# Attention and a squared-ReLU layer on one core: a buffer of its own for the last adds, GpSimd's copy behind the next sums, and DMA turns that hold back loads

## The chip, the core and the metric

The kernel runs on one core of a Trainium2 chip. Its engines are TensorE (PE; its weight loads are shown as PEld), VectorE (DVE), ScalarE (ACT), GpSimd (POOL) and SyncE (SP, which here only issues DMAs). The metric is the device time of one execution in microseconds; before the change the median of three executions was 402.41 us (402.33 to 403.97).

## The reference

Eight batches of 384 tokens go through grouped-query attention (16 query heads, 4 key/value heads, head size 64), and the result through two dense layers with a squared ReLU between them.

```python
scores = scale * np.matmul(q, k.transpose(0, 1, 3, 2))
attn = np.exp(scores - np.max(scores, axis=-1, keepdims=True))
attn = attn / (np.sum(attn, axis=-1, keepdims=True) + 1e-09)
x = np.matmul(attn, v).transpose(0, 2, 1, 3).reshape(B * S, H * D)   # 3072 x 1024
h = np.maximum(x @ w_in, 0.0)                                        # w_in 1024 x 2048
return h * h @ w_out                                                 # w_out 2048 x 1024
```

## The kernel before, in words

**A planner writes the program.** The Python code keeps a `Recorder` (lines 9 to 145). Every operation is added with the keys that it reads and writes and with an estimated cost; the recorder keeps a clock for each engine and derives the semaphore waits. The main loops (from line 1701 for batches 0 and 1, from line 1856 for the others) look at these clocks and choose what TensorE does next. Before each choice `upkeep` (line 1624) looks which side work is due: loads, DMA turns, sums, squares, output writes. So the order of every queue comes from estimated times, and a changed estimate can change the order of later work.

**The stages of a batch.** Loads of k, q and v go through POOL's queue (`load_k`, `load_q`, `load_v`). SP issues DMA transposes ("turns") of k and q (`turn_k_half`, `turn_q_dma`). Scores come in bursts of matmuls (line 448), ACT applies exp (line 458), TensorE multiplies by v (line 515), DVE divides by the sum (lines 528 and 530), and a DMA turn of the outputs (`turn_o_dma`, line 533) makes `xT`, the input of the dense layers. For batches 2 to 7 both dense layers use seven block products in place of eight (Strassen). DVE makes the sums of `xT` that this needs (`sums`, line 649, instructions at line 658); then TensorE runs the upward products (line 902) while the attention of the next batch goes between them. The results are added on DVE (line 886), and squared into `h2T` by ACT (lines 788, 796) or by POOL (line 800, in `close_squares`).

**The downward products.** Rows of 128 tokens are paired. Each batch has three such rows; two make pair "A", and the third one is paired with the third row of the batch before (pair "D" of the odd batches). For that, POOL copies the third row's part of `h2T` into `h2x` in batches 2, 4 and 6 (line 1199, queued in `d_q` by `sum_ops`, line 1151; `d_q` is a queue in order). Each pair runs seven products (line 944, in `pair_of`). As products end, `done` (line 1108) evicts them: `copied` makes a copy on ACT (line 1094) or DVE (line 1095), `added` adds on DVE (line 1101), and at product 7 POOL adds two buffers, `p5 += a3` (line 1133). `put` queues the output's DMA on SP (line 1308). The buffers `y_sb` are slots handed out in turn by `y_slot`. In the last pair the products end in the order 7, 4, 3, and product 3 runs as `whole_product` (line 999): first 384 columns, then 128.

**Pacing.** For batches above 3, `dma_at` holds the time before which no further load piece (2.0 after the one before) or turn of k, v or q (3.5 after) may be issued (lines 1651 and 1660). The turns of outputs are not paced.

**DVE and POOL.** An operation with `port=True` is one for which the planner charges more when POOL is at work (line 87): it adds the time by which the two overlap, over POOL's last four operations. `w2_q` (line 1692) places the scaling and the sums of the second weight matrix (lines 1226, 1231, 1238) on DVE or ACT as their planned clock is within `lead` of TensorE's.

Of the kernel before, what the change touches and what calls it, by code (L numbers as in the profile page):

```python
# [8 lines left out]
class Recorder:  # L9
# [36 lines left out]
    def add(self, eng, fn, reads=(), writes=(), dma=None, cost=0.1, issue=0.1, shared=(), after=(), port=False):  # L46
        i = len(self.ops)
        deps = self.deps_of(reads, writes)
        raw = {self.writer[r] for r in reads if r in self.writer}
        for r in reads:  # L50
            self.readers.setdefault(r, []).append(i)
        for w in writes:
            self.writer[w] = i
            self.readers[w] = []
        need = set(after)
        for d in deps:
            o = self.ops[d]
            if o["dma"] is None and o["eng"] == eng and dma is None:
                if eng in self.IN_ORDER or d not in raw:
                    continue  # L60
            need.add(d)
        if dma is not None:
            if dma in self.dma_last:
                need.add(self.dma_last[dma])
            self.dma_last[dma] = i
        start = max([self.clock[eng]] + [self.ops[d]["end"] for d in need])
        if dma is not None:
            self.clock[eng] = start + issue
            if eng == "gpsimd":
                self.pool.append((start, start + 0.3 * issue))  # L70
            q = eng
            begin = max(self.ring.get(q, 0.0), start + issue + 0.8)
            if shared and begin > start + issue + 0.8:
                shared = (3.0, shared[1])
            if shared and self.ring.get("gpsimd", 0.0) > begin:
                self.ring["gpsimd"] += shared[1]
                for o in self.ops:
                    if o["eng"] == "gpsimd" and o["dma"] is not None and o["end"] > begin:
                        o["end"] += max(0.0, min(shared[1], o["end"] - 1.2 - begin))
                cost = shared[0]  # L80
            self.ring[q] = begin + cost
            end = begin + cost + (1.5 if begin > 30 else 1.2 if eng == "gpsimd" else 0.7)
        else:
            if eng == "gpsimd":
                self.pool.append((start, start + cost))
            elif port:
                cost += 1.0 * sum(max(0.0, min(z, start + cost) - max(a, start)) for a, z in self.pool[-4:])
            self.clock[eng] = start + cost
            end = start + cost + (0.2 if eng == "tensor" else 0.07)
        self.ops.append(dict(eng=eng, fn=fn, dma=dma, need=need, signal=False, start=start, end=end))  # L90
        return i
# [57 lines left out]
def bass_gqa_attention__then__ffn_squared_relu_kernel(  # L149
# [619 lines left out]
    def close_squares(which):  # L769

        for x in [x for x in open_squares if which(x)]:
            open_squares.remove(x)
            i, r, dst, keys, relu, b = x
            assert b < FAST or b in ranged
            val = hr[r]
            two = val.rearrange("p (f t) -> p f t", f=2)
            end = R.ops[i]["end"]
            act, dve, pool = [max(R.clock[e], end) for e in ("scalar", "vector", "gpsimd")]
            slack = 1.5 * (b >= FAST and keys[0][1:] not in LAST_SQUARES)
            plans = [(act + 0.45 * (1 + relu) + slack, "ss"), (max(act + 0.52 * relu, pool) + 0.77 + 0.2, "sg")]  # L780
            if relu:
                plans.append((pool + 2.2 + 0.6, "gg"))
            elif not ff["now"]:
                plans.append((dve + 0.95 + 0.4, "sv"))
            one, other = min(plans)[1]
            to, by = small(b)
            if relu and one == "s":
                R.add("scalar", lambda e, val=val, to=to: e.activation(val, val, AF.Relu, scale=to),  # L788
                      reads=[("hr", r)] + by, writes=[("hr", r)], cost=0.54 if by else 0.45)
            elif relu:  # L790
                R.add("gpsimd", lambda e, val=val, to=to: e.tensor_scalar(val, val, to, 0.0, ALU.mult, ALU.max),
                      reads=[("hr", r)] + by, writes=[("hr", r)], cost=1.42)
            for _, c, t in keys:
                wrote[c, t] = b
            if other == "s":
                R.add("scalar", lambda e, dst=dst, two=two: e.activation(dst, two, AF.Square),  # L796
                      reads=[("hr", r)], writes=keys, cost=0.45)
            else:
                eng = dict(g="gpsimd", v="vector")[other]
                n = R.add(eng, lambda e, dst=dst, two=two: e.tensor_tensor(dst, two, two, ALU.mult),  # L800
                          reads=[("hr", r)], writes=keys, cost=0.77 if other == "g" else 0.95, port=other == "v")
                if other == "v":
                    hr_read[r] = (n,)

# [249 lines left out]
    def pair_of(b, pair, one, two):  # L1054
# [28 lines left out]

        ys = {}
        g1, g2 = b_1 % 3, b_2 % 3

        def slot(name):
            ys[name] = y_slot(b)
# [15 lines left out]
        def put(who, x, name, c0=0, c1=512):  # L1104
            bb, i3 = who
            send(bb, i3, 512 * x + c0, 512 * x + c1, ys[name], c0)

        def done(prod, at, *cols):
            flags.add(("done", b, pair, prod))
            if prod == 1:  # L1110
                copied(at, "a1", g1)
            elif prod == 2:
                added(at, g1, "a1", "a1")
                put(one, 0, "a1")
            elif prod == 5:
                copied(at, "p5", g2)
                ys["bank"] = at
            elif prod == 6:
                eng = copied(at, "a2", g2)
                if g1 != g2:  # L1120
                    copied(at, "b2", g1, eng)
                else:
                    ys["b2"] = ys["a2"]
                if b == B - 1 and pair == "D":
                    added(ys["bank"], g1, "b2", "b2", TAIL, 512, (R.writer[("y", ys["p5"])],))
            elif prod == 7:
                if g1 == g2:
                    slot("a3")
                else:
                    ys["a3"] = ys["a2"]  # L1130
                added(at, g2, "a2", "a3")
                y, z = ys["a3"], ys["p5"]
                R.add("gpsimd", lambda e: e.tensor_tensor(y_sb[z], y_sb[z], y_sb[y], ALU.add),
                      reads=[("y", y), ("y", z)], writes=[("y", z)], cost=1.28)
                put(two, 1, "p5")
            elif prod == 3:
                added(at, g1, "b2", "b2", *cols)
                put(one, 1, "b2", *cols)
            else:
                added(at, g2, "a3", "a3")  # L1140
                put(two, 0, "a3")

        def product(prod, at):
            (a, na), (w, nw) = left(prod), right(prod)
# [6 lines left out]
    def sum_ops(b, double):  # L1151
# [40 lines left out]
        if double:  # L1192
            for n, prod in ((0, 5), (1, 6), (3, None), (2, 3)):
                reads, go = op("D", n, None)
                d_q.append((lambda prod=prod: prod is None or ("done", b, "A", prod) in flags, reads, go, True))
        elif b < B - 1:
            keys = [("h2T", c, 1) for c in range(NFC)] + [("DS", b, "A", n, x) for n in (2, 3) for x in range(2)]
            d_q.append((lambda: all_wrote(range(NFC), (1,)), keys, lambda: R.add(
                "gpsimd", lambda e: e.tensor_copy(h2x[:, :, :], h2_16[:, :, 256:384]), reads=keys,
                writes=[("h2x", b), ("h2x", b - 2)] + X_OVER, cost=2.0), True))  # L1200

# [325 lines left out]
    def below():  # L1527
        return not ff["tiles"] and not ff["now"]
# [95 lines left out]
    def upkeep(now):  # L1624
# [66 lines left out]
            add_sums(b)  # L1691
        while w2_q and w2_q[0][0]() and R.when(reads=w2_q[0][1], eng="none") <= now:
            eng = w2_q[0][3]
            lead = {"scalar": 0.6 if ff["b"] == 1 else 0.1, "vector": 0.5 if ff["b"] == FAST and not below() else -9 if m_q or lazy else 0.6 if below() else 0.9 if ff["b"] == 1 else 0.1}
            able = [x for x in ("vector", "scalar") if eng in (x, "any") and R.clock[x] <= now + lead[x]]
            if not able:
                break
            w2_q.pop(0)[2](*(able[:1] if eng == "any" else ()))
# [157 lines left out]
    while ff["now"] or ff["tiles"] or ff["down"]:  # L1856
# [60 lines left out]
        elif what[2] == "av2":  # L1917
# [7 lines left out]
                    m_q.append((b, lambda b=b: widest_of(b)))  # L1925
            if c % 2 == 1:
                turn_o_dma(b, c // 2)
                x_done[b] += 2
        elif what[2] == "top":
            n, then = spread_q.pop(0)  # L1930
# [39 lines left out]
```

## Time and profile before

| what | value |
|---|---|
| median of three executions | 402.41 us |
| the profiled execution's own time | 402.27 us |
| its span, first to last instruction | 400.3 us |
| PE busy | 389.6 us (97%) |
| DVE busy | 315.4 us (79%) |
| ACT busy | 266.7 us (67%) |
| POOL busy | 148.4 us (37%) |
| granted TensorE clock | 0.999 |

The span leaves out 1.97 us of the profiled execution's own time, which lie before the first or after the last instruction. In rows of the timeline the first number is the start in microseconds from the span's beginning, the second the duration; x2 means that two such instructions are merged into one row, and what stands in square brackets is the engine's idle time before it and what ended it. A matmul's end is modelled, and TensorE works on several at a time, so that "busy" is not the same as full speed.

### The profile page before, as it was taken

The page shows a single profiled execution, that of the slowest core. Times are in us where ns is not written, and L with a number is a line of the kernel's source. Part 1 is how long each engine was busy: PE and PEld are TensorE (multiplying, and loading weights), DVE is VectorE, ACT ScalarE, POOL GpSimd, SP SyncE. Part 2 cuts the span into 40 slices and gives each one's busy share as a digit, 9 for nine tenths or more (in the row PEclk, how much of TensorE's full clock was granted, in tenths as well). Part 3 has the DMA queues.
Part 4 walks back from the last instruction along what each step waited for, and adds up shares of the span by engine and source line. Part 5 has one row for each costly group of instructions (what it writes and reads, how often), then busy time and mean ns, then how long its engine had stood idle before and what let it go on. Part 6 is the DMA issues. An engine that isn't in the chain of part 4 may idle for free.

```text
span 400.3 us, 15645 instructions
## 1 busy us (share of the span) xinstructions
PE 389.6 (97%) x7022; PEld 300.2 (75%) x7022; DVE 315.4 (79%) x652; ACT 266.7 (67%) x390; POOL 148.4 (37%) x169
## 2 busy tenths in 40 slices
PE   9999999999999999999999999998999999999995
PEld 6565764555666897588977999698987899789653
DVE  3689879899898987987987788986885688856644
ACT  6948999596655897768675587877783297426510
POOL 8665510245001664355332343444301144126111
PEclk9999999999999999999999999999999999999999
DMA  9999999995329873398597816697622223120022
GB/s 174 189 199 182 207 185 190 208 165 80 43 75 189 133 86 60 76 179 91 99 120 161 162 23 92 81 149 109 70 60 93 92 44 25 48 80 4 28 81 104
DMA packets 95634, 44.39 MB, mean 111 GB/s; under 512 B 75984, under 2 KB 89552, under 8 KB 95568
## 3 DMA queue, kind: packets, MB, share of 16 engines
q0 software_dynamic: 36672, 17.44, 35.6%
q1 hardware_dynamic: 58224, 25.47, 31.9%
q8 instruction: 55, 0.90, 1.0%
q10 hardware_dynamic: 672, 0.49, 0.4%
q14 instruction: 11, 0.09, 0.1%
HBM read 35.65 MB, written 12.58 MB: 121 GB/s over the span
## 4 chain that ended last, share of the span: by engine, by line
PE 78%; DVE 7%; DMA 7%; issue 4%; POOL 3%; ACT 1%; POOLq 0%; ACTq 0%; DVEq 0%
PE ps L944 27%; PE ps L902 26%; PE ps L515 6%; PE ps L448 6%; PE ps L611 6%; DMA w_in_sb<-in_moe_w_in_dram 5%; PE ps L1276 5%; DMA wx<-in_k_dram 1%; PE ps L474 1%; DVE w_out_sb L1226 1%; POOL w_in_sb L320 1%; DVE hr L624 1%; DVE y_sb L1101 1%; DVE w_out_sb L1238 1%; ACT h2T L796 1%
## 5 line engine op out<-in xcount | busy, mean ns | idle before, releaser
L458 ACT ACTIVATE expT<-ps 128x1024 bf16<-128x1024 f32 (+1 forms) x124 | 120.8, 1015 | 25.3 <-PE ps L448 25.2
L944 PE MATMUL ps<-w_out_sb,h2T 64*128 64x512 f16 x528 | 97.8, 376 | 0.5 <-DVE y_sb L1101 0.5
L902 PE MATMUL ps<-xT,w_in_sb 64*128 64x192 f16 x1152 | 84.8, 243 | 0.3 <-DVE y_sb L1101 0.3
L902 PEld LDWEIGHTS ps<-xT,w_in_sb 64*128 64x128 f16 x1152 | 71.2, 94 | 3.5 <-DVE y_sb L1101 0.5
L800 POOL TENSOR_TENSOR h2T<-hr 128x384 f16<-128x384 f32 x54 | 44.6, 845 | 51.7 <-ACT hr L788 51.6
L944 PE MATMUL ps<-area,xT 64*128 64x512 f16 x288 | 55.8, 376 | 0.0
L944 PEld LDWEIGHTS ps<-w_out_sb,h2T 64*128 64x128 f16 (+1 forms) x528 | 41.1, 94 | 15.8 <-DVE y_sb L1101 0.6
L448 PE MATMUL ps<-qT,kT 64*128 64x256 bf16 (+2 forms) x336 | 51.4, 326 | 0.6 <-ACT expT L458 0.4
L902 PE MATMUL ps<-s_all,wx 64*128 64x192 f16 x768 | 51.9, 242 | 0.0
L788 ACT ACTIVATE hr<-hr,bits 128x384 f32<-128x384 f32 x71 | 41.9, 609 | 11.8 <-DVE hr L886 11.5
L886 DVE TENSOR_TENSOR hr<-ps,hr 128x384 f32<-128x384 f32 x72 | 39.2, 555 | 9.4 <-PE ps L902 6.2
L902 PEld LDWEIGHTS ps<-s_all,wx 64*128 64x128 f16 x768 | 44.4, 94 | 0.9
L515 PE MATMUL ps<-v_aug,expT 64*128 64x65 bf16 x1680 | 43.7, 190 | 1.2 <-issue 0.6
L611 PE MATMUL ps<-xT,w_in_sb 64*128 64x384 bf16 x448 | 42.1, 323 | 1.0 <-DVE hr L624 0.6
L1101 DVE SCALAR_TENSOR_TENSOR y_sb<-ps,bits,y_sb 128x512 f32<-128x512 f32 (+2 forms) x38 | 26.9, 724 | 19.9 <-PE ps L944 13.3
L515 PEld LDWEIGHTS ps<-v_aug,expT 64*128 64x128 bf16 x1680 | 39.3, 94 | 2.7 <-DVE o_sb L530 0.7
L944 PE MATMUL ps<-area,h2T 64*128 64x512 f16 x144 | 36.4, 376 | 0.0
L1094 ACT ACTIVATE y_sb<-ps,bits 128x512 f32<-128x512 f32 x20 | 13.6, 687 | 33.7 <-PE ps L944 33.6
L878 ACT COPY hr<-ps 128x384 f32<-128x384 f32 x34 | 16.2, 479 | 27.2 <-PE ps L902 26.6
L611 PEld LDWEIGHTS ps<-xT,w_in_sb 64*128 64x128 bf16 x448 | 22.0, 94 | 16.2 <-DVE hr L624 1.8
L902 PE MATMUL ps<-s_all,w_in_sb 64*128 64x192 f16 x384 | 32.8, 243 | 1.3 <-issue 1.3
L902 PE MATMUL ps<-xT,wx 64*128 64x192 f16 x384 | 33.2, 243 | 0.7 <-issue 0.6
(147 smaller groups left out, 748.6 us busy)
## 6 DMA issues: line engine op xcount, KB each, us to landing
out_dram<-y_sb SPq DMA_DIRECT2D x45, 256.0 KB, 2.4
w_in_sb<-in_moe_w_in_dram POOLq DMA_DIRECT2D x8, 512.0 KB, 15.1
w_out_sb<-in_moe_w_out_dram POOLq DMA_DIRECT2D x4, 1024.0 KB, 28.9
q_st<-in_q_dram POOLq DMA_DIRECT2D x19, 192.0 KB, 5.2
q_st<-in_q_dram POOLq DMA_DIRECT2D x4, 384.0 KB, 23.1
k_st<-in_k_dram POOLq DMA_DIRECT2D x6, 192.0 KB, 4.1
k_st<-in_v_dram POOLq DMA_DIRECT2D x5, 192.0 KB, 5.0
wx<-in_q_dram POOLq DMA_DIRECT2D x2, 384.0 KB, 8.4
```

Of the source, the lines that this page charges most:

```text
L448: mm = pe.matmul(ps[:, base + x, m * wide:(m + 1) * wide], kT[at(b)][64 * x:64 * x + 64, u, :], q_cols(b, u // NJ, x, c0, c0 + wide))
L458: R.add("scalar", lambda e: e.activation(dst, src, AF.Exp, scale=0.125), reads=keys, writes=[("expT", slot(b, u), t) for u, _, _ in pieces ...
L515: m = pe.matmul(ps[:, p[x], n * DP:n * DP + D + 1], w, v_aug[b % 2][r, g * NJ + j, 0:D + 1], start=(n + j + y == 0), stop=(n + j + y == 2 ...
L611: m = pe.matmul(bank(4 + xs[x])[:, 0:S], w_in_sb[r, kc, c * 128:(c + 1) * 128], xT[b % NXT][r, kc, :], start=(phase < 2 and kc == 0), stop ...
L788: R.add("scalar", lambda e, val=val, to=to: e.activation(val, val, AF.Relu, scale=to), reads=[("hr", r)] + by, writes=[("hr", r)], cost=0. ...
L800: n = R.add(eng, lambda e, dst=dst, two=two: e.tensor_tensor(dst, two, two, ALU.mult), reads=[("hr", r)], writes=keys, cost=0.77 if other ...
L878: R.add("scalar", lambda e: e.copy(hr[r][:, :], src), reads=[("bank", at)], writes=[("hr", r)], cost=0.45, after=hr_read.pop(r, ()))
L886: R.add("vector", lambda e: e.tensor_tensor(hr[r][:, :], src, hr[r][:, :], ALU.add), reads=[("bank", at), ("hr", r)], writes=[("hr", r)], ...
L902: return lambda pe: pe.matmul(bank(at)[:, f * h:f * h + h], w[r, kc, c:c + 128], m[r, kc, :], start=(prod in (1, 5, 2) and y + f + kc == 0 ...
L944: return lambda pe: pe.matmul(bank(p.at)[:, 0:512], p.a(k, r), p.w(k, r), start=start, stop=stop, skip_group_check=True)
L1101: R.add("vector", lambda e: e.scalar_tensor_tensor(y_sb[z][:, c0:c1], bank(at)[:, c0:c1], gs[g], y_sb[y][:, c0:c1], ALU.mult, ALU.add), re ...
L1276: m = pe.matmul(bank(i)[:, 0:n], h2T[:, c, i3 * 128:(i3 + 1) * 128], w_out_sb[:, c, c0:c1], start=(c == 0), stop=(c == NFC - 1))
```

## The change

Six things change, all in the planner's code.

1. The charge for `port=True` operations (line 87): instead of the overlap with POOL's last four operations it is the rest of that POOL operation (of the last six) which is running when the DVE operation starts.
2. A square on POOL or DVE gets a wait on earlier instructions of the same engine that read the part of `h2T` which it overwrites.
3. In the last pair alone (`last`): the two copies at product 6 go to ACT, and the add of product 4 writes a new slot `a4` and no longer overwrites `a3`, which POOL's add reads.
4. The copy into `h2x` becomes due only when the sums of the next batch are made.
5. `lead` for `w2_q` on DVE in batch 1 falls from 0.9 to 0.5 while the upward products run.
6. In the loop for batches 2 to 7, each turn of outputs moves `dma_at` to at least 3.5 after TensorE's clock, so that no load piece and no paced turn follows earlier.

```diff
@@ Recorder.add
             elif port:
-                cost += 1.0 * sum(max(0.0, min(z, start + cost) - max(a, start)) for a, z in self.pool[-4:])
+                cost += max([0.0] + [z - start for a, z in self.pool[-6:] if a <= start < z])
@@ close_squares
                 n = R.add(eng, lambda e, dst=dst, two=two: e.tensor_tensor(dst, two, two, ALU.mult),
-                          reads=[("hr", r)], writes=keys, cost=0.77 if other == "g" else 0.95, port=other == "v")
+                          reads=[("hr", r)], writes=keys, cost=0.77 if other == "g" else 0.95, port=other == "v",
+                          after=tuple(d for key in keys for d in R.readers.get(key, ()) if R.ops[d]["eng"] == eng))
@@ pair_of
+        last = b == B - 1 and pair == "D"
...
-                eng = copied(at, "a2", g2)
+                eng = copied(at, "a2", g2, "scalar" if last else None)
...
-                if b == B - 1 and pair == "D":
+                if last:
                     added(ys["bank"], g1, "b2", "b2", TAIL, 512, (R.writer[("y", ys["p5"])],))
...
-                added(at, g2, "a3", "a3")
-                put(two, 0, "a3")
+                ys["a4"] = slot("a4") if last else ys["a3"]
+                added(at, g2, "a3", "a4")
+                put(two, 0, "a4")
@@ sum_ops
-            d_q.append((lambda: all_wrote(range(NFC), (1,)), keys, lambda: R.add(
+            d_q.append((lambda: b + 1 in summed and all_wrote(range(NFC), (1,)), keys, lambda: R.add(
                 "gpsimd", lambda e: e.tensor_copy(h2x[:, :, :], h2_16[:, :, 256:384]), reads=keys,
@@ upkeep
-            lead = {"scalar": 0.6 if ff["b"] == 1 else 0.1, "vector": 0.5 if ff["b"] == FAST and not below() else -9 if m_q or lazy else 0.6 if below() else 0.9 if ff["b"] == 1 else 0.1}
+            lead = {"scalar": 0.6 if ff["b"] == 1 else 0.1, "vector": 0.5 if ff["b"] == FAST and not below() else -9 if m_q or lazy else 0.6 if below() else 0.5 if ff["b"] == 1 else 0.1}
@@ loop for batches 2 to 7
                 turn_o_dma(b, c // 2)
+                dma_at[0] = max(dma_at[0], R.clock["tensor"] + 3.5)
                 x_done[b] += 2
```

## The prediction

> **What bounds the kernel now.** I read the page first: the span, the busy times, and the chain of work that ended last.
>
> ```profile
> span 400.3 us, 15645 instructions
> PE 389.6 (97%) x7022; PEld 300.2 (75%) x7022; DVE 315.4 (79%) x652; ACT 266.7 (67%) x390; POOL 148.4 (37%) x169
> PE 78%; DVE 7%; DMA 7%; issue 4%; POOL 3%; ACT 1%; POOLq 0%; ACTq 0%; DVEq 0%
> ```
>
> TensorE is busy for 389.6 of 400.3 us, and the change takes no matmul away. So what can be won is mostly the 10.7 us in which TensorE does nothing. Asked for by window, the last stretch holds almost half of them.
>
> ```profile
> 371.00:401.00 30.00, 25.05 (x233) 14.33 (x228) 14.19 (x24) 6.22 (x11) 3.12 (x3) 0.97 0.20 71
> ```
>
> The first number behind the stretch is its length, the second PE's busy time: 4.95 us without work, of which 0.7 lie past the span's end. For the rest I asked whom PE waited for (total us, times, longest).
>
> ```profile
> PE ps L902 <- issue: 2.0, 2, 1.3
> PE ps L611 <- DVE hr L624: 0.6, 2, 0.4
> PE ps L515 <- issue: 0.6, 1, 0.6
> PE ps L515 <- DVE o_sb L530: 0.5, 1, 0.5
> PE ps L944 <- DVE y_sb L1101: 0.5, 1, 0.5
> ```
>
> So the middle has two kinds of holes: 2.6 us of "issue", where PE waits for nothing that the profile shows, and 1.6 us behind a late DVE. Anything else that the change moves is under a busy PE.
>
> **Part 3, the last pair.** This is the end of the timeline, with the issue times of the output DMAs and the adds by form.
>
> ```profile
> 393.52 1.03 DVE L1101 SCALAR_TENSOR_TENSOR y_sb<-ps,bits,y_sb 128x128 f32<-128x128 f32 x2
> 394.13 1.92 PE L999 MATMUL ps<-w_out_sb,xT 128*128 128x384 f16 x16
> 394.63 1.27 POOL L1133 TENSOR_TENSOR y_sb<-y_sb 128x512 f32<-128x512 f32 x1 [10.82 <-DVE y_sb L1101]
> 395.92 2.64 SPq L1308 DMA_DIRECT2D out_dram<-y_sb  x4
> 396.00 1.73 DVE L1101 SCALAR_TENSOR_TENSOR y_sb<-ps,bits,y_sb 128x512 f32<-128x512 f32 x3 [1.45 <-POOL y_sb L1133]
> L1101 DVE SCALAR_TENSOR_TENSOR y_sb<-ps,bits,y_sb 128x384 f32<-128x384 f32 x1 | 0.6, 609 | 0.0
> L1308 SPq DMA_DIRECT2D out_dram<-y_sb x4: 332/332/432, 395.9 to 398.1; - x4
> ```
>
> DVE is free at 394.55 but waits 1.45 us until POOL has read `a3`; then three adds run one after the other until 397.73 (0.75 for the whole width, 0.61 for 384 columns, the rest, some 0.35, for 128), and the last DMA is issued by 398.56. With a slot of its own the add of product 4 starts at about 394.6 and ends at 395.3. The 384-column add follows its matmuls, whose share of the 1.92 us is 384/512, 1.44: it runs from about 395.6 to 396.2. The last add comes after all matmuls (396.05) and that one: 396.2 to 396.55, 1.2 us earlier than 397.73. On SP the output of `a4` is ready first (395.3), then POOL's (395.9), then the other two: three issues of 0.33 and one of 0.43 behind 395.92 at most, so that the last ends at about 397.0 in place of 398.56, 1.5 us earlier. The same 768 KB then leave in less time, so I take **-1.4**. Bounds: -0.9 if POOL's output is issued ahead of `a4` and all four issues take 0.43 (395.92 + 1.73 = 397.65, against 398.56), and -1.55.
>
> This needs DVE's add to run beside POOL's. An earlier pair shows just that.
>
> ```profile
> 382.55 1.26 POOL L1133 TENSOR_TENSOR y_sb<-y_sb 128x512 f32<-128x512 f32 x1 [10.96 <-DVE y_sb L1101]
> 383.44 0.75 DVE L1101 SCALAR_TENSOR_TENSOR y_sb<-ps,bits,y_sb 128x512 f32<-128x512 f32 x1 [0.98 <-PE ps L944]
> 390.35 0.69 ACT L1094 ACTIVATE y_sb<-ps,bits 128x512 f32<-128x512 f32 x1 [2.77 <-PE ps L944]
> 392.07 1.41 DVE L1095 TENSOR_SCALAR y_sb<-ps,bits 128x512 f32<-128x512 f32 x2 [2.70 <-PE ps L944]
> ```
>
> The add begun at 383.44 took 0.75, its usual time, while POOL worked until 383.81. The two copies moved to ACT cost twice 0.69 in place of 1.41 and end at the same time; ACT's row behind it shows 2.77 us of idle time, so they cost **0**. Without that cover the first add would be late by what they take longer.
>
> **Part 4, the copy behind the sums.** Batch 4's copy lies like this.
>
> ```profile
> 252.91 1.90 POOL L1199 COPY area<-h2T 128x2048 f16<-128x2048 f16 x1
> 253.07 1.83 DVE L675 CAST top_w<-bits 128x128 bf16<-128x128 f32 x1
> 254.82 0.74 DVE L1101 SCALAR_TENSOR_TENSOR y_sb<-ps,bits,y_sb 128x512 f32<-128x512 f32 x1
> L675 DVE CAST top_w<-bits x14: 226/227/1829, 57.6 to 346.6; 128x128 bf16<-128x128 f32 x14
> ```
>
> The cast takes 0.227 as a rule and 1.83 here, to the end of the copy. The add of line 1101 behind it comes 1.6 us late, and PE waits 0.5 for that add. Behind the sums the cast has long run, and the next squares come only with the next upward products. I take **-0.5**, the whole wait. Who waits for the copy: POOL's own queue (q loads, `p5` adds) and pair D's first products, more than a batch's upward products later. In batch 2 it can hit something new:
>
> ```profile
> 167.59 0.55 DVE L658 TENSOR_TENSOR s_all<-xT,s_all 128x768 f16<-128x768 f16 x1
> 168.90 1.25 POOL L1133 TENSOR_TENSOR y_sb<-y_sb 128x512 f32<-128x512 f32 x1 [0.47 <-DVE y_sb L1101]
> 169.03 1.21 DVE L675 CAST top_w<-bits 128x128 bf16<-128x128 f32 x1
> ```
>
> A copy from 168.2 would keep this cast until 170.1, or, with POOL's add behind it, until 171.4; now it ends at 170.24. The scale that hangs on it is needed only at the seventh piece of the next upward products, so I count 0, with +0.6 as the upper bound.
>
> **Parts 1 and 5, DVE's planned clock.** Two places with several `port` operations in a row (the first in batch 1, where `lead` is changed, the second in batch 2):
>
> ```profile
> 88.80 4.37 DVE L1226 TENSOR_SCALAR w_out_sb<-w_out_sb,bits 128x1024 f16<-128x1024 bf16 x6
> 135.73 2.55 DVE L1238 TENSOR_TENSOR w_out_sb<-w_out_sb 128x1024 f16<-128x1024 f16 x2
> 135.75 1.99 POOL L338 COPY k_dup<-k_st 128x1536 bf16<-128x1536 bf16 x1
> ```
>
> The six of line 1226 hold DVE until 93.17, and one of the two waits for line 624 quoted above ends behind them. The two sums of line 1238 took 2.55 us, since the second stood until POOL's copy ended at 137.74. The old charge can at most double such an operation; the new one charges the whole rest, as the cast above shows it. With that and the smaller `lead`, fewer of them are put ahead of the adds that PE waits for. The price is in the waits quoted first: 0.6 for line 624 and 0.5 for line 530, 1.1 in all. The operations have to go somewhere, so I take a third, **-0.4**, with -1.1 and +1.1 (as much again in new places) as bounds.
>
> **Part 6, the held-back loads and turns.** The largest "issue" hole, with the DMAs ahead of it; of a window's last two numbers the first is the mean busy share of the DMA engines, which passes 1 where queues overlap.
>
> ```profile
> 266.46 2.06 SPq L535 DMA_TRANSPOSE xT<-o_sb  x1
> 267.34 0.74 POOL L302 DMA_DIRECT2D k_st<-in_v_dram  x1 [3.91 <-PE ps L448]
> 270.80 1.70 SPq L362 DMA_TRANSPOSE qT<-q_st  x1
> 270.00:272.00 2.00, 2.00 (x62) 1.93 (x58) 1.66 (x4) 1.08 (x3) 0.29 (x1) 1.00 1.36 238
> 273.31 1.33 issue
> q8 instruction: 55, 0.90, 1.0%
> ```
>
> PE stops in the middle of one product without a semaphore, in a stretch where a turn of outputs, a load and a turn of q overlap. Its instructions come by DMA too (55 packets, 0.90 MB), and I read the hole as instructions that came late. With the hold, the load at 267.34 (0.9 us after the turn) moves back by up to 2.6 us, and the q turn behind it by as much. That may free this hole, but the loads then meet the next fetch. I take about a quarter of 2.6, **-0.6**; the bounds are -2.6 and +1.3, one more hole of the longest kind. In its section "Queues, rings and completion order" the Trainium skill's page "DMA: Bandwidth & Descriptors" says that a DMA engine takes turns between its queues packet by packet; by that a fetch waits for a few packets and not for whole transfers, and the hold would win nothing here (a rival below). No row here settles it.
>
> **Part 2, waits of POOL on itself,** cost **0**: what they wait for, POOL's own sums and copies of the batch before, ended long ago, and POOL sits idle for 51.7 us ahead of these squares.
>
> ```profile
> L800 POOL TENSOR_TENSOR h2T<-hr 128x384 f16<-128x384 f32 x54 | 44.6, 845 | 51.7 <-ACT hr L788 51.6
> ```
>
> All 54 could start 0.95 later (51.7 / 54) and that idle time would still take it, in the mean.
>
> **The sum**: -1.4 - 0.5 - 0.4 - 0.6 = -2.9. The profiled execution took 402.27, so 399.4; the median of the runs is 0.14 above it, which gives **399.5**.
>
> **The rivals.** *The end alone.* The plan is made anew, and the holes in the middle only change places: -1.4, or -1.9 with the cast, 400.5 to 401.0. For it speaks that the middle's holes are small and follow from chance meetings; against it that the cast and the doubled sums have a plain cause. *The holds win nothing at the "issue" holes:* instructions are late for a reason of their own, since two of the three holes are only 0.6 long and stand in other stretches; then -2.3, 400.1. *The holds eat the slack (slower).* Batch 5's first q turn is issued at 187.34 and its first exp runs at 201.85.
>
> ```profile
> 187.34 1.86 SPq L362 DMA_TRANSPOSE qT<-q_st  x1
> 201.85 1.94 ACT L458 ACTIVATE expT<-ps 128x1024 bf16<-128x1024 f32 x2 [1.25 <-PE ps L448]
> DMA to landing us min/median/max: 3.7/4.0/4.3
> ```
>
> With 4.0 us to land, 10.5 us are free. Four turns of outputs per batch hold 3.5 each, 14 at most; past 10.5 the scores come late and PE has nothing to put between the downward products. At 14 that is 3.5 us in batch 5, and 402.4 - 1.4 + 3.5 = 404.5, more if later batches follow. Against it: most turns lie closer together with what follows than 3.5, but a hold runs at the same time as the 2.0 and 3.5 that are kept already. *The change does not do what it says.* If the add of product 4 still ends behind POOL's, the end wins 0.2 at most, and all else is chance: 402.
>
> **How the numbers follow.** I count 0.5% (2.0 us) as what can be told from no change: below 400.4 is faster, above 404.4 slower. The forecast case has 0.38 (its own range is 397.0 to 400.4), the holds without gain 0.12, the end alone 0.28, the holds that eat the slack 0.15, the change without effect 0.07. Faster is the first two, 0.50; same is 0.28 + 0.07 less 0.02 for new holes that cost more, 0.33; slower 0.17. The range reaches from 397.0, where the fetch term and the clock term are near their lower bounds, to 403.5, which takes in the rivals but the holds in full.
>
> **What would show it.** Right: DVE's add of product 4 begins near 394.6 on the old scale, with no wait for POOL at line 1101, and the span ends some 1.4 us sooner after the last matmul than now; no cast over 0.3 beside line 1199; "issue" under 2.6 in PE's waits; fewer doubled sums at lines 1226 to 1238. Wrong: a new row in PE's waits behind exp or `qT`, or "issue" holes of the same total elsewhere.

## The result, and the profile after

The changed kernel took 399.41 us (median of 6 runs, 398.96 to 401.24) against 402.37 of the kernel before on the same chip (6 runs): a ratio of 0.9932, 95% interval 0.9908 to 0.9956, or 3.0 us less. The prediction was 399.5.

The profiled execution is the longest of these six, 401.24. The same kernel was profiled a second time, at 399.02; its span there is 397.2. Of the runs in the table further down, one (405.94, with the copy alone) lies 1.6% above the shortest of its kernel, at a granted clock of 0.992, and is left out. First the page of the changed kernel: span, busy times, chain of work.

```profile
span 399.4 us, 15634 instructions
PE 388.2 (97%) x7019; PEld 298.7 (75%) x7022; DVE 313.1 (78%) x645; ACT 272.4 (68%) x398; POOL 147.6 (37%) x168
PE 85%; DMA 7%; DVE 3%; POOL 2%; issue 1%; ACT 1%; POOLq 0%; DVEq 0%
```

TensorE bounds it as before; DVE's and issue's shares of the chain fell from 7% to 3% and from 4% to 1%. Most of the 4% was no idle time of TensorE: the chain of the kernel before ended through POOL's last add, and 10.79 us of "issue" at 383.81 are POOL's time ahead of it. Whom PE waited for (total us, times, longest), in the changed kernel:

```profile
PE ps L903 <- issue: 2.4, 3, 1.1
PE ps L448 <- ACT expT L458: 1.5, 4, 0.5
PE ps L611 <- DVE hr L624: 0.9, 2, 0.7
```

and in the second profile of it:

```profile
PE ps L448 <- ACT expT L458: 1.7, 5, 0.5
PE ps L903 <- issue: 0.6, 2, 0.4
```

Three things are to be seen. Two waits of 0.5 each are gone, that of line 515 behind line 530 and that of the downward products behind the add of line 1101 (now 1103). The wait behind exp has grown from 0.4 to 1.5 and 1.7. And two executions of one program differ by 1.8 us in the "issue" row alone, where their times differ by 2.2: these holes make up most of the difference between these two, so a single profile says little about them.

The end of the changed kernel, in the timeline and by its output writes:

```profile
392.21 1.27 ACT L1096 ACTIVATE y_sb<-ps,bits 128x512 f32<-128x512 f32 x2 [1.04 <-PE ps L945]
393.51 2.02 DVE L1103 SCALAR_TENSOR_TENSOR y_sb<-ps,bits,y_sb 128x128 f32<-128x128 f32 x3 [4.00 <-ACT y_sb L1096]
394.26 1.92 PE L1000 MATMUL ps<-w_out_sb,xT 128*128 128x384 f16 x16
394.77 1.27 POOL L1135 TENSOR_TENSOR y_sb<-y_sb 128x512 f32<-128x512 f32 x1 [10.82 <-DVE y_sb L1103]
395.77 1.07 DVE L1103 SCALAR_TENSOR_TENSOR y_sb<-ps,bits,y_sb 128x384 f32<-128x384 f32 x2 [0.25 <-PE ps L1000]
L1311 SPq DMA_DIRECT2D out_dram<-y_sb x4: 332/332/450, 395.6 to 397.2; - x4
DMA to landing us min/median/max: 1.8/2.0/2.2
```

The third of the three adds merged at 393.51 is that of product 4; it runs beside POOL's add and waits for nothing. The last matmuls end at 396.18 and the span at 399.4: 3.2 us, against 4.2 before (396.05 and 400.3). The longer stretch that the prediction began with now reads

```profile
371.00:401.00 30.00, 25.18 (x235) 14.68 (x231) 13.07 (x22) 7.63 (x13) 3.26 (x3) 0.98 0.20 72
```

4.82 us without PE's work, of which 1.6 lie past the span's end (0.7 before).

### The profile page after: what moved, and what is told of

The parts are those of the page before. It is cut to its first block, busy times and chain, and to the rows that moved or that the text cites. A ratio compares the mean times of both kernels' runs of the same rounds, so it can differ in the third digit from the quotient of the medians.

```text
span 399.4 us, 15634 instructions
## 1 busy us (share of the span) xinstructions
PE 388.2 (97%) x7019; PEld 298.7 (75%) x7022; DVE 313.1 (78%) x645; ACT 272.4 (68%) x398; POOL 147.6 (37%) x168
## 4 chain that ended last, share of the span: by engine, by line
PE 85%; DMA 7%; DVE 3%; POOL 2%; issue 1%; ACT 1%; POOLq 0%; DVEq 0%
PE ps L945 32%; PE ps L903 28%; PE ps L515 7%; PE ps L448 6%; PE ps L611 5%; DMA w_in_sb<-in_moe_w_in_dram 5%; PE ps L1279 5%; DMA area<-in_v_dram 1%; DVE hr L624 1%; PE ps L474 1%; DVE w_out_sb L1229 1%; POOL w_in_sb L320 1%; ACT expT L458 1%; DVE y_sb L1103 0%; POOL q_st L309 0%
## 5 line engine op out<-in xcount | busy, mean ns | idle before, releaser
L945 PE MATMUL ps<-w_out_sb,h2T 64*128 64x512 f16 x528 | 96.2, 376 | 0.0
L800 POOL TENSOR_TENSOR h2T<-hr 128x384 f16<-128x384 f32 x50 | 40.5, 829 | 47.1 <-ACT hr L788 46.9
L945 PE MATMUL ps<-area,xT 64*128 64x512 f16 x288 | 54.3, 376 | 0.0
L448 PE MATMUL ps<-qT,kT 64*128 64x256 bf16 (+2 forms) x336 | 50.4, 324 | 1.8 <-ACT expT L458 1.5
L945 PEld LDWEIGHTS ps<-w_out_sb,h2T 64*128 64x128 f16 (+1 forms) x528 | 38.7, 94 | 17.2 <-ACT h2T L796 0.3
L515 PE MATMUL ps<-v_aug,expT 64*128 64x65 bf16 x1680 | 42.7, 190 | 0.1
L1096 ACT ACTIVATE y_sb<-ps,bits 128x512 f32<-128x512 f32 x24 | 16.3, 687 | 38.1 <-PE ps L945 35.2
L1135 POOL TENSOR_TENSOR y_sb<-y_sb 128x512 f32<-128x512 f32 x9 | 12.1, 1346 | 79.5 <-DVE y_sb L1103 79.5
```

Of the source, the lines that this page charges most:

```text
L448: mm = pe.matmul(ps[:, base + x, m * wide:(m + 1) * wide], kT[at(b)][64 * x:64 * x + 64, u, :], q_cols(b, u // NJ, x, c0, c0 + wide))
L515: m = pe.matmul(ps[:, p[x], n * DP:n * DP + D + 1], w, v_aug[b % 2][r, g * NJ + j, 0:D + 1], start=(n + j + y == 0), stop=(n + j + y == 2 ...
L945: return lambda pe: pe.matmul(bank(p.at)[:, 0:512], p.a(k, r), p.w(k, r), start=start, stop=stop, skip_group_check=True)
```

## The experiments

All ratios are to the kernel before on the same chip; 1% is 4.0 us, and gains in us below are worked out from the ratios.

| kernel | median us (runs) | before us | ratio, 95% interval |
|---|---|---|---|
| end alone (part 3) | 401.32 (12) | 402.15 | 0.9981, 0.9957 to 1.0004 |
| hold alone (part 6) | 403.43 (12) | 402.15 | 1.0032, 1.0008 to 1.0055 |
| plan alone (parts 1, 5) | 403.10 (12) | 402.15 | 1.0011, 0.9984 to 1.0037 |
| copy alone (parts 4, 2) | 400.70 (9) | 402.15 | 0.9960, 0.9939 to 0.9981 |
| all, second profile | 399.00 (6) | 402.38 | 0.9930, 0.9905 to 0.9955 |
| all but the hold | 399.76 (12) | 402.38 | 0.9947, 0.9925 to 0.9969 |
| copy and end, early write | 401.52 (12) | 402.38 | 0.9986, 0.9960 to 1.0011 |
| before, small loads and turns | 397.92 (5) | 402.38 | 0.9912, 0.9883 to 0.9940 |
| before, small turns alone | 401.14 (12) | 401.94 | 0.9978, 0.9957 to 1.0000 |
| plan and hold | 400.18 (12) | 401.94 | 0.9945, 0.9923 to 0.9967 |
| all, third write by itself | 399.34 (8) | 401.94 | 0.9943, 0.9921 to 0.9966 |
| all, hold of 7.0 | 434.28 (6) | 401.94 | 1.0791, 1.0759 to 1.0823 |

### The parts one by one

The end alone:

```diff
+                ys["a4"] = slot("a4") if last else ys["a3"]
+                added(at, g2, "a3", "a4")
+                put(two, 0, "a4")
```

> The kernel before with part 3 alone (the last pair's copies on ACT, the add of product 4 into a slot of its own). My theory: only the end changes, and the span ends about 1.0 us sooner after the last matmul than before (4.25 us before, 3.2 us in the changed kernel's profile), so the time falls by 0.9 to 1.4 us. The rival that the end wins next to nothing, because the outputs then leave in a bunch, expects less than 0.4 us.

The median went down by 0.8, the ratio's interval reaches from -1.7 to +0.2. In its trace the span ends 3.2 us after the last matmul, as in the whole change, against 4.2 before: the traces show a gain of 1.0 at the tail, smaller than the 1.4 forecast, which the runs alone do not tell from nothing.

The hold alone:

```diff
                 turn_o_dma(b, c // 2)
+                dma_at[0] = max(dma_at[0], R.clock["tensor"] + 3.5)
```

> The kernel before with part 6 alone (each turn of outputs of batches 2 to 7 holds back loads and paced turns by 3.5). My prediction gave -0.6 us (fewer holes of the 'issue' kind). Rival one, the holes come whatever the loads do: 0 +-0.5. Rival two, the holds eat the slack: over +1 us, with waits for exp or for qT in PE's list.

It made the kernel slower, by 1.3 (0.3 to 2.2). Its profiled execution is its shortest of twelve (401.67), and even that has one "issue" hole of

```profile
PE ps L515 <- issue: 1.6, 1, 1.6
```

The exp wait stays at 0.4 here, so late scores are not what it paid for. Part of the 1.3 is a lower granted clock in 7 of its 12 runs (below, under "Do the parts add up?").

The plan alone (the new charge and the lead):

```diff
+                cost += max([0.0] + [z - start for a, z in self.pool[-6:] if a <= start < z])
...
-  else 0.9 if ff["b"] == 1 else 0.1}
+  else 0.5 if ff["b"] == 1 else 0.1}
```

> The kernel before with parts 1 and 5 alone (the charge for DVE operations beside POOL, the smaller lead in batch 1). My prediction gave -0.4 us, by fewer waits of PE for lines 624 and 530 (1.1 us before). The rival that the new plan only moves the holes expects 0, and the waits for DVE as long as before in other places.

No gain in the median: +0.4 (-0.6 to +1.5), with a lower granted clock in 8 of its 12 runs (below). In its trace the wait behind line 530 is gone, but the one behind line 624 has grown from 0.6 to 0.9, and there is an "issue" row of 2.7:

```profile
PE ps L902 <- issue: 2.7, 2, 2.5
PE ps L611 <- DVE hr L624: 0.9, 2, 0.7
```

The copy alone:

```diff
-            d_q.append((lambda: all_wrote(range(NFC), (1,)), keys, lambda: R.add(
+            d_q.append((lambda: b + 1 in summed and all_wrote(range(NFC), (1,)), keys, lambda: R.add(
```

> The kernel before with parts 4 and 2 alone (the copy into h2x due only after the next sums; POOL's waits on itself). My prediction gave -0.5 us. The profile of the changed kernel speaks for a rival: POOL's queue runs ahead of the plan, nothing in the program makes the copy wait for the sums, and so it starts when POOL is free; then it lies at the same place as before (about 252.9 in batch 4, beside the cast) and the time stays within 0.3 us.

It gained 1.6 (0.8 to 2.5), more than the 0.5 of the hole. This is the group of casts and batch 4's copy in its timeline:

```profile
L675 DVE CAST top_w<-bits x14: 226/227/228, 56.2 to 345.4; 128x128 bf16<-128x128 f32 x14
252.78 0.23 DVE L675 CAST top_w<-bits 128x128 bf16<-128x128 f32 x1
257.04 0.55 DVE L658 TENSOR_TENSOR s_all<-xT,s_all 128x768 f16<-128x768 f16 x1
259.16 1.90 POOL L1200 COPY area<-h2T 128x2048 f16<-128x2048 f16 x1
```

The copy runs behind the sums, no cast is held up, and the wait of PE for line 1101's add has gone. In the changed kernel the same places look like this:

```profile
252.18 0.68 DVE L1183 TENSOR_TENSOR xT<-h2T,xT 128x1024 f16<-128x1024 f16 x1
252.93 1.89 POOL L1202 COPY area<-h2T 128x2048 f16<-128x2048 f16 x1 [4.67 <-DVE xT L1183]
254.02 0.88 DVE L675 CAST top_w<-bits 128x128 bf16<-128x128 f32 x1
256.75 0.54 DVE L658 TENSOR_TENSOR s_all<-xT 128x768 f16<-128x768 f16 x1
```

The copy starts 3.8 us *ahead* of the sums. The edit moves its place in POOL's queue, and no wait ties it to the sums; with the hold, the loads that stood ahead of it in that queue come later, so POOL reaches the copy as soon as the last sum of line 1183 is there. Without the hold (all but the hold, below) it lies behind the sums again, at 258.94, and the longest cast takes 0.255. The cast still meets it, for 0.88 in place of 1.83, because the copy now begins 0.07 us behind that sum, where before it began 1.0 behind it (252.91, and the sum's end at 251.92). That is short enough: PE no longer waits for the add behind it. For this part 4 is not needed. The plan with the hold (below) has no part 4, and its copy too begins 0.07 us behind the last sum (250.33 + 0.68), its longest cast is the same, and the downward products' wait of 0.5 behind line 1101 is gone there too:

```profile
250.33 0.68 DVE L1180 TENSOR_TENSOR xT<-h2T,xT 128x1024 f16<-128x1024 f16 x1
251.08 1.89 POOL L1199 COPY area<-h2T 128x2048 f16<-128x2048 f16 x1 [4.67 <-DVE xT L1180]
252.17 0.88 DVE L675 CAST top_w<-bits 128x128 bf16<-128x128 f32 x1
```

### Do the parts add up?

The four ratios give -0.8, +1.3, +0.4 and -1.6, together -0.7; the whole gives -2.8. So parts were put together.

> The changed kernel once more, for a second profile and to stand beside the next three on one chip. Expected: -2.7 us +-1 against the kernel before; its waits of PE behind exp (1.5 us near 168 in the first profile) belong to the plan and come again at the same place, while the 'issue' holes near 186, 196 and 275 come at the same places with other lengths.

The wait behind exp came again near 168. Of the "issue" holes of the first profile, the one near 186 did not, the one near 195 came with 0.37 in place of 0.90, and the one near 274 with 0.2 in place of 1.05.

> The changed kernel without part 6 (no hold behind the turns of outputs). If the hold costs what it cost alone (+1.3 us), this is faster than the changed kernel by 0.5 to 2 us. If it pays only together with the other parts (the prediction's -0.6), this is slower than the changed kernel by 0.5 or more. With POOL's loads back ahead of the copy in its queue, the copy of batch 4 should then lie behind the cast again, as it does with part 4 alone.

All but the hold is at 0.9947, where the sum of its parts by themselves is -2.0, 0.9950: these three add up. With the hold it is 0.9930. The intervals overlap, so this pair alone doesn't show that the hold is worth anything; the spread of the runs is narrower with it (398.42 to 399.12 in six, against 397.94 to 401.37 in twelve).

The pair that shows a difference is the plan without and with the hold:

> Parts 1, 5 and 6 alone, without the end and the copy. Theory, hold and new plan gain together though each alone gained nothing: the median is that of the whole change plus what the end (1.0) and the copy's hole (0.5) are worth, about 400.5. Rival, the parts add up as measured one by one (+0.4 and +1.3): 403.5 to 404.

Each of them alone was no faster than before; together they are faster by 2.2 (1.3 to 3.1), and the interval lies clear of that of the plan alone. Added up they would be 1.7 slower. Its waits:

```profile
PE ps L448 <- ACT expT L458: 1.7, 5, 0.5
PE ps L902 <- issue: 1.0, 1, 1.0
```

It has the new wait behind exp, which neither part shows alone (0.2 to 0.4 in both), and less "issue" than either. So the two medians do not add up.

Most of that gap goes with the clock. For every run the mean granted clock is on record, the share of its full clock that TensorE got:

| kernel | runs at 0.996 or less | their median | median of the others |
|---|---|---|---|
| before, beside the first four rows | 0 of 33 | | 402.15 |
| hold alone | 7 of 12 | 404.28 | 402.46 |
| plan alone | 8 of 12 | 403.61 | 400.93 |
| before, beside plan and hold | 3 of 25 | 404.49 | 401.62 |
| plan and hold | 0 of 12 | | 400.18 |

One profile has a mean of 0.996, that of the end alone (403.71). An "issue" hole of 2.29 us ends there at 183.56, and from 184.82 on the clock is at 0.50 for 3.41 us. The third number from the end is the clock:

```profile
181.30:183.50 2.20, 0.00 (x0) 0.00 (x0) 0.40 (x1) 1.44 (x3) 1.69 (x3) 1.00 1.03 85
185.00:188.00 3.00, 3.00 (x39) 3.00 (x37) 1.87 (x4) 1.76 (x3) 1.62 (x2) 0.50 0.41 41
```

At half the clock 3.41 us lose 1.7, which is 0.4% of the run, as the mean says. Not every such hole brings this: behind the one of 2.50 of the plan alone, the clock stays at 1.00. Among the runs without it the plan is 1.2 faster than before, the hold 0.3 slower, and both together are 1.4 faster. That is near a sum, but the groups are small and chosen by what came of them, so no part's price is shown by it. What the pair has and neither part alone has is a trace without a hole from 172 to 184, where the plan alone has its 2.50 and the hold alone its 1.6. Why the two together avoid it was not found out.

### What makes the "issue" holes

The kernel before, with a quarter of the rows in each load of k, v and q and one block in each turn of k and q, in batches 4 to 7 only:

```diff
-            q_st[st][:, h0:h1, :],
+            q_st[st][:, h0:h0 + 1 if b > 3 else h1, :],
...
-            out=qT[at(b)][:, 12 * half:12 * half + 12, :],
+            out=qT[at(b)][:, 12 * half:12 * half + (1 if b > 3 else 12), :],
...
```

> The kernel before with the same plan and the same instructions, but of batches 4 to 7 each load of k, v and q brings only a quarter of its rows and each turn of k and q turns only one block of 6 or 12: what these batches compute is left wrong, the turns of outputs and all else is as before. If the 'issue' holes come from instructions that wait behind loads and turns, the holes near 177, 182 and 274 (2.6 us together in the profile before) go and the time falls by 1.5 to 3 us. If a fetch is late for its own reasons (queues served in turn, packet by packet), the holes stay and the time stays within 0.5 us.

The kernel leaves out most of the input of these batches, so it only serves to time the rest. It took 3.5 us less (2.4 to 4.7), and no "issue" row is left in PE's waits. The order of every engine's instructions is that of the kernel before, so only the DMA traffic differs. PE's busy time in the middle, first before and then with small loads and turns (stretch, its length, PE's busy time; the last two numbers are the DMA share and GB/s):

```profile
160.00:280.00 120.00, 117.00 (x2512) 99.22 (x2512) 98.49 (x216) 86.00 (x119) 50.30 (x56) 1.00 0.73 112
```

```profile
160.00:280.00 120.00, 119.87 (x2627) 102.84 (x2625) 101.28 (x222) 87.88 (x122) 48.13 (x58) 1.00 0.31 65
```

2.9 us of PE's idle time have gone; 2.5 of them are the three "issue" holes (0.56, 0.65 and 1.33), and the wait of 0.5 behind line 1101 has gone too. What comes late can be seen in the DMA queues of 6 us ahead of the largest hole (packets, MB, share of 16 engines). In the kernel before, from 266 to 272:

```profile
q1 hardware_dynamic: 1849, 0.92, 92.2%
q0 software_dynamic: 589, 0.22, 35.7%
...
k_st<-in_v_dram POOLq DMA_DIRECT2D x1, 192.0 KB, 7.0
xT<-o_sb SPq DMA_TRANSPOSE x1, 7.7
qT<-q_st SPq DMA_TRANSPOSE x1, 4.7
```

With small loads and turns, the same stretch:

```profile
q0 software_dynamic: 144, 0.05, 9.5%
q1 hardware_dynamic: 315, 0.06, 6.4%
q8 instruction: 2, 0.03, 2.9%
...
xT<-o_sb SPq DMA_TRANSPOSE x1, 2.8
```

Two instruction packets (queue q8) pass with small loads, none in the kernel before. That kernel runs some us behind by then, so the packets are better compared by their number: both kernels have 55, and the 37th starts at 272.32 in the kernel before, 6.6 us after the 36th (265.71), and at 266.56 with small loads, 4.3 after it (262.25). It comes 2.3 us later than there. It ends at 273.30, and PE, which stops at 273.31, goes on at 274.64, 1.3 us behind that end. The same is seen at all 22 "issue" holes of over 0.3 us in the twelve traces that have one: each ends 1.3 to 1.6 us after the end of this queue's last packet, and it is always the 21st, 22nd, 23rd, 25th or 37th packet. PE's other waits of that size end anywhere from 1.1 to 7.4 us after one. So the holes are instructions that come late. The transfers themselves are slowed too: the turn of outputs needs 7.7 in place of 2.8 to land.

In those 6 us each packet of q1 took 48 ns on its engine (92.2% of 16 engines over 6 us, by 1849 packets), so that 2.3 us are some 48 of them. Whether that breaks the rule of the Trainium skill in the prediction is not settled, since no run here shows how many of the profile's packets make one of the page's. The Trainium skill's page "Runtime: NRT & Kernel Launch", section "Instruction fetch mechanics", calls the cost of such a fetch mostly hidden. The trace of before agrees for 52 of its 55 packets; the other three left the holes.

Loads or turns? The kernel before with the turns alone cut:

```diff
-            out=qT[at(b)][:, 12 * half:12 * half + 12, :],
+            out=qT[at(b)][:, 12 * half:12 * half + (1 if b > 3 else 12), :],
```

> This is the kernel before, with the DMA turns of k and q in batches 4 to 7 cut to a sixth and a twelfth of their blocks; all loads keep their size. The output of those batches is not that of the reference. Theory, TensorE's instructions come late mainly behind the turns: the 'issue' rows in PE's waits fall under 0.5 in all, and the median is near that of the run with small loads and small turns, about 398. Rival, they come late mainly behind the loads: 'issue' stays at 1.5 to 3.5, and the median within 0.7 of before. If both count alike, about 400.

It gained 0.9 (0.0 to 1.7), a quarter of the 3.5, and "issue" is between the two:

```profile
PE ps L902 <- issue: 0.9, 1, 0.9
PE ps L515 <- issue: 0.6, 1, 0.6
```

So by difference the loads on POOL's queue weigh most, or loads and turns together (loads cut alone were not run).

### A longer hold

```diff
-                dma_at[0] = max(dma_at[0], R.clock["tensor"] + 3.5)
+                dma_at[0] = max(dma_at[0], R.clock["tensor"] + 7.0)
```

> All six parts, with a hold of 7.0 in place of 3.5 behind each turn of outputs. Theory, more distance between turns and loads lets the instructions come in time: 'issue' under 0.5, the median 0.3 to 0.8 below that of the whole change. Rival, the distance is already enough and longer holds make loads and scores late: new or longer waits of PE behind exp (line 458, now 1.5 to 1.7) or qT, the median 1 or more above that of the whole change.

This is the prediction's slower rival, and far dearer than it was priced: 32 us more than before.

```profile
PE 406.9 (94%) x7022; PEld 298.3 (69%) x7022; DVE 321.2 (74%) x653; ACT 268.9 (62%) x386; POOL 150.0 (35%) x172
PE ps L903 <- DVE y_sb L1103: 6.5, 4, 2.5
PE ps L448 <- DMA qT<-q_st: 2.1, 1, 2.1
370.00:380.00 10.00, 6.67 (x129) 4.43 (x131) 5.39 (x16) 3.88 (x4) 0.00 (x0) 0.50 0.21 41
380.00:390.00 10.00, 8.12 (x101) 6.86 (x98) 5.65 (x12) 1.41 (x3) 0.82 (x1) 0.51 0.14 53
```

"Issue" is no longer among PE's waits, as hoped, but batch 4's first turn of q is issued at 162.68 (146.60 in the changed kernel) and PE waits 2.1 for it; from there the attention runs late and PE waits for DVE. PE's idle time is 25.6 us against 8.4 in the second profile of the changed kernel (388.8 busy of 397.2). The rest of the loss goes with the clock: in the two stretches shown, where PE has holes, the granted clock is 0.50 and 0.51. Over the whole run it is at 0.50 in four stretches, 37.5 us together, which at half the clock lose 18.8; PE's busy time is 18 us longer for the same matmuls. So somewhere between 3.5 and 7.0 lies an edge. The wait behind exp at 3.5 (1.5 to 1.7) may be a first sign of it; that was not tested.

### The last writes

Two kernels ask what sets the end. The first has copy and end but the plan before, and records the write of the 384 columns early, ahead of its neighbours:

```diff
                 put(one, 1, "b2", *cols)
+                if last:
+                    put_away(lambda y: True)
```

> The kernel before with parts 2, 3 and 4, without the charge, the lead and the hold; and the last output's first 384 columns are sent as soon as their add is done, not after the add of the last 128 (the two get keys of their own). If the parts add up: -1.6 (part 4 alone) -0.8 (part 3 alone) -0.3 (the last DMA is issued 0.37 us earlier), so -2.7 or better, at least as fast as the whole change. If the gain of the whole change hangs on the new plan: only about -1.5.

The second is the whole change, with the third write waiting for its own add and not for the last one:

```diff
-                  reads=[("bank", at), ("g", g), ("y", y)], writes=[("y", z)], cost=0.68 if c1 - c0 > 128 else 0.27, after=after)
+                  reads=[("bank", at), ("g", g), ("y", y)], writes=[("yz" if c0 and not after else "y", z)], cost=0.68 if c1 - c0 > 128 else 0.27, after=after)
...
-                            reads=[("y", yb)], writes=[("out", b, i3, c0)]
+                            reads=[("yz" if y0 else "y", yb)], writes=[("out", b, i3, c0)]
```

> All six parts, and the third of the last four output writes waits for its own add only (384 columns), no longer for the last add behind it on DVE. Theory, this wait is what part 3 fell short by: SP issues the third write near 0.45 earlier and the fourth near 0.35 earlier, the span ends 2.8 to 2.9 after the last matmul's end in place of 3.23, and the median is 0.3 to 0.4 below that of the whole change. Rival, the end hangs on how long the last writes take to land and not on their issue: 3.2 as before, and no difference.

The first gained nothing that can be told from no change (-0.6; -1.6 to +0.4); five of its twelve runs have a mean granted clock of 0.995 or 0.996. Its first write is issued only 0.1 ahead of the last matmul's end (394.75 and 394.88), as in the kernel before, and its span ends 3.7 after that end. In the second the last issue ends at 395.61, 1.21 behind the last matmul (394.40), in place of 1.52 in the changed kernel (397.70 and 396.18); and yet the span (397.6) ends 3.2 behind it, as without the edit, and the ratio is that of the whole change. Its row of the adds, and its writes:

```profile
393.99 1.07 DVE L1103 SCALAR_TENSOR_TENSOR y_sb<-ps,bits,y_sb 128x384 f32<-128x384 f32 x2 [0.25 <-PE ps L1000]
393.77 1.84 SPq L1314 DMA_DIRECT2D out_dram<-y_sb  x4
L1314 SPq DMA_DIRECT2D out_dram<-y_sb x4: 332/396/459, 393.8 to 395.2; - x4
DMA to landing us min/median/max: 2.1/2.2/2.4
```

The last write is issued 0.3 sooner and takes 0.3 longer to land: the rival was right. From the first issue to the last landing it is 3.5 (393.8 to 395.2 + 2.1), and 3.4 in the changed kernel (395.6 to 397.2 + 1.8), the shortest landing being that of the last and smallest write. In the kernel before, with gaps between the issues, it was 3.9 (395.9 to 398.1 + 1.7, by the same view). To the nearest hundredth it is 3.44 to 3.46 in all six traces with close issues (end alone, both profiles of the whole change, all but the hold, and these two), and 3.92 before. The landings of the changed kernel show why: they come at 397.63, 398.31, 398.80 and 399.01, that is 0.68, 0.49 and 0.21 apart for the second, third and fourth write of 256, 192 and 64 KB. The second and the third thus left at some 390 GB/s, one behind the other.

## Why the prediction was right, and where only its sum was

**Part 3, -1.4: the mechanism right, the size too large.** The add of product 4 ran beside POOL's as said, and the copies on ACT cost nothing. The tail gained 1.0. The step that failed is "the same 768 KB then leave in less time": I measured the end by the last issue, and behind it the writes' landing became the limit. The last issue, too, came only 1.0 sooner (1.52 behind the last matmul in place of 2.51), since the third write waits for the last add; without that wait it came 1.3 sooner (1.21), and the end stayed. As it is worded, the sum of the prediction is off as well: three issues of 0.33 and one of 0.43 behind 395.92 end at 397.3, and 397.0 takes the first of them to go at 395.3. Four writes issued close together need some 3.5 us from the first issue to the last landing, so what counts is when the *first* can go (0.1 ahead of the last matmul's end before, 0.6 after: 0.5 us) and that the gaps close (3.9 to 3.4 or 3.5, another 0.4 to 0.5).

**Part 4, -0.5: the wait went, not by the step named.** "Behind the sums the cast has long run" holds in the copy alone; there the gain was even 1.6, of which the trace explains 0.5; the rest is not explained. In the whole change the copy runs ahead of the sums, and "no cast over 0.3 beside the copy" was wrong: 0.88. The wait went since the copy starts sooner and the cast meets only its second half, and the plan with the hold does that without part 4. So the 0.5 of this term can't be put down to part 4 in the whole change.

**Parts 1 and 5, -0.4: not shown.** By themselves they gave +0.4 (-0.6 to +1.5); the four of the twelve runs without the lower clock lie 1.2 below before, too few to count on. Of the two waits that the term was a third of, the one behind line 530 went and the one behind line 624 grew by 0.3. "Fewer of them are put ahead" came true in batch 2 alone: at line 1241, the former 1238, the longest sum fell from 1.95 to 1.42; in batch 1, at line 1229, the former 1226, DVE has 13 scalings in place of 14 and the longest stayed at 1.68.

```profile
L1241 DVE TENSOR_TENSOR w_out_sb<-w_out_sb x4: 680/702/1424, 134.1 to 138.6; 128x1024 f16<-128x1024 f16 x4
L1229 DVE TENSOR_SCALAR w_out_sb<-w_out_sb,bits x13: 471/478/1679, 83.0 to 97.6; 128x1024 f16<-128x1024 bf16 x13
```

**Part 6, -0.6: the cause right, the size not shown.** That the holes are instructions that come late behind loads and turns is shown by the small loads and by the packets at the holes. But the median with the hold rose by 1.3 on the kernel before; it fell by about 2.7 on the new plan (0.9945 against 1.0011), and by about 0.7 on all the rest, within the error. The term priced a hole by its length alone. The runs show that a hole can also bring 3.41 us at half the clock, 1.7 more, in some kernels in most runs and in others in none, and a single trace of the kernel before, at 0.999, could not tell that.

**Part 2** was not tried apart from the copy.

**The sum.** -2.9 was forecast and -3.0 measured, but the agreement is better than the terms, and its closeness is luck. The end gave 0.4 less than forecast, and plan and hold together, forecast at -1.0, gave -2.2. Behind exp there is a new wait of 1.5, one of the signs given for "wrong".

**The rivals.** *The end alone* (400.5 to 401.0) lies above the measured median; the interval of the ratio reaches up to 400.6. *The holds win nothing* fell by its reason: with small loads and turns the instructions are no longer late, so it is not for a reason of their own. By its number, 400.1, it can't be excluded, since that lies within the interval. *The holds eat the slack* is real at 7.0, and may show in the 1.5 us behind exp at 3.5; it was placed at batch 5, and at 7.0 it began at batch 4. *The change without effect* fell with the add of product 4.

## What to carry to other kernels

Where a queue's order comes from planned times, the price of a pacing edit that was read off one trace did not carry over to another plan: measure it together with the plan that it will run in, and try both sides of its size, since with 3.5 the whole is 3 us faster than before and with 7.0 it is 32 us slower. Before medians of such kernels are compared, the granted clock of every run belongs beside them: it split the runs of two parts in two groups, 1.8 and 2.7 us apart. For a tail of several output writes, count from the first issue to the last landing, not to the last issue. And an operation put later in a queue is later only if what stands ahead of it stays late; if it must come behind other work, it needs a wait.

## What the runs showed of the hardware that was not expected

TensorE's own instructions come through the DMA engines in pieces of 16 KB (0.90 MB in 55 packets), and with bulk traffic in flight a piece can come so late that PE stands still: 2.5 us in the middle of this kernel, none with small loads. PE went on 1.3 to 1.6 us after the end of such a packet, at all 22 holes. The "issue" total went from 0.6 to 2.4 in two executions of one program.

A half-clock stretch of 3.41 us followed 1.3 us behind the end of a hole of 2.29 (the end alone), and none followed one of 2.50 (the plan alone). Where holes of some 2 us followed each other (the hold of 7.0), the granted clock stood at 0.50 for 20 us; the changed kernel's mean is 1.000. Late buffers went with 17 us more of idle time and 18 us more of slower work, so that they cost about twice the time that PE stood idle. That the holes caused the lower clock was not tested by itself.

Four output writes issued within 1.7 us took 3.44 to 3.46 us from the first issue to the last landing, whether the last one was issued 1.35 or 1.69 us behind the first.
